# Longformer attention into a softplus MLP on one core: the second batch's v cast by its own transfers, heads paired by neighbours, and a new written-out order

## The chip, the cores and the metric

The kernel runs on one core of one Trainium2 chip. The metric is the device time of one execution in microseconds; lower is better. Five engines work side by side, each through its own instructions in order: PE (TensorE, matmuls; PEld is its weight load), DVE (VectorE), ACT (ScalarE), POOL (GpSimd) and SP (SyncE, which here only issues transfers). ACT and POOL issue transfers too. They wait for each other through semaphores.

## The reference

q, k and v have 8 batches, 8 heads, 576 tokens and 64 columns (fp32). Attention sees a window of 32 tokens to either side, and 8 global tokens that see and are seen by all. The result, put back to 4608 rows of 512, goes through a two-layer MLP with softplus.

```python
scores = scale * np.matmul(q, k.transpose(0, 1, 3, 2))
mask = np.abs(pos[:, None] - pos[None, :]) <= window
mask = mask | is_global[:, None] | is_global[None, :]
attn = softmax(np.where(mask, scores, -1e9))
x = np.matmul(attn, v).transpose(0, 2, 1, 3).reshape(B * S, H * D)
h = x @ w_in                                   # 512 -> 2048
g = np.maximum(h, 0.0) + np.log1p(np.exp(-np.abs(h)))
return g @ w_out                               # 2048 -> 512
```

## The kernel before

**Tiling.** A batch has 18 blocks of 32 queries. Four blocks make a pair-group `n` (36 in all), four groups make a stage `m` of 512 tokens (9 stages). For each group the kernel computes scores (`s`, L1077), the row maximum, the exponentials on ACT, the sum and its reciprocal, the normalised weights `pn` (L1132) and their 32x32 transposes `pt` (L1141). Once per batch the 8 global queries are scored against all keys (`sg`, L968) and applied to all values (`ov`, L997), which gives the global rows `vg`. `xo` (L1251) multiplies the weights by v, transposed, and its copies to `xT` are the MLP's input: `h` (L1286, with `w_in`, tiles `win`), softplus to `g` on ACT (L1292), and `o` (L1297, with `w_out`, tiles `wout`). The copies of all kinds share the helper at L720.

**The first two batches** (`EARLY = 2`) are loaded in parts of 256 tokens in their natural layout (`load_part`, parts t = 0, 1 and a tail of 64 tokens), rounded to bf16 (`kb`, `qb`), and transposed on PE (`tr`, with `pick`, which collects the global tokens). Block `a` of such a transpose holds head `a` on partitions 0 to 63 and head `a + 4` on 64 to 127. Later batches use layouts that DVE transposes. Stage 0's values are computed in three pieces (groups 0; 1 and 2; 3), so that the MLP can start after the first.

**Array tiles.** A score matmul is 64x32: row group `g` (64 rows), column quarter `quad(a)`. Row group 0 writes one PSUM bank and row group 1 another:

```python
for a_ in range(HG):
    for g in range(2):
        a = a_ ^ g
        nc.tensor.matmul(out=PS["s", n, g][quad(a), x, :], lhsT=qx[b % 2][rows(g), a, ...], ...)
```

So eight matmuls in a row use eight different tiles of the array. `ov` of batch 0 takes its 32-row quarters to four tiles on the array's diagonal, all into one bank; `ov` of the later batches has eight tiles and two banks.

**Loads.** SP issues q and k, and v from batch 1 on. POOL issues the transfers that cast fp32 to bf16: v of batch 0, `w_in` (four tiles of three transfers each), `w_out` (four). Two one-element transfers named `trail` make SP wait: the first for the lower half of `win2`, the second for `wout0`; what stands behind them on SP starts no earlier. v of batch 1 goes to `stage2` in fp32 and is rounded to `vb1` by a copy on ACT and one on POOL.

**What sets the order.** The class `_Order` holds all pieces of work with their dependencies. A table of numbers, `ORDER`, says piece by piece which comes next and on which engine; the class's costs only date them. Where its dates leave PE idle before `WARM`, it puts in `warm` matmuls on zeros (L729), for a share `FILL` of the gap.

Of the kernel before, what the change touches and what calls it, by code (L numbers as in the profile page):

```python
# [20 lines left out]
class _Order:  # L21
# [23 lines left out]
    def stall(self, t, took, ins):  # L45

        held, n = 0, self.issued
        asked, need, due, last = self.fetch
        due = list(due)
        while n + ins >= min(asked, need):  # L50
            at = min(asked, need)
            here = t + held + took * max(at - n, 0) / max(ins, 1)
            if at == asked:
                due.append(here)
                asked += self.BLOCK
            else:
                ask = due.pop(0)
                took_ = max(next(x for until, x in self.SLOW if ask < until), self.backlog(ask + 1200) - ask + 2400)
# [48 lines left out]
    BEGIN = 3450  # L107
    PACKETS = {1: 1024, 2: 256, 4: 576, 8: 1152}

    def settle(self, dma):  # L110
# [5 lines left out]
        while any(at[q] < len(lines[q]) for q in range(2)):  # L116
            on = []
            for q in range(2):
                if at[q] < len(lines[q]):
                    t = max(lines[q][at[q]][1], last[q])  # L120
# [30 lines left out]
    FILL, FILLT, NARROW, NFILL, NFILLT = 0.55, 220, 0, 0.8, 140  # L151
# [49 lines left out]
    def run(self, free):  # L201
# [16 lines left out]
        while ready:  # L218
# [57 lines left out]
            if j["moves"]:  # L276
                mine = "POOL" if "POOL" in j["cost"] else "SP"
                dma.append((mine, t + 1500 if j["cost"][e][0] else t, j["moves"], j))
# [28 lines left out]
def kernel(  # L307
# [45 lines left out]
    PARTED = range(4)  # L353
    LEAD = 800
# [137 lines left out]
    EARLY = 2  # L492

    hot = const([P, len(PARTS), NG], BF16, "hot")
    HD = H * D

    def flat(x):
        return x[:].rearrange("p x y z -> p (x y z)")
# [976 lines left out]
```

## Time and profile before

| | |
|---|---|
| median of 3 runs | 335.49 us (334.19 to 336.04) |
| the profiled execution | 333.06 us, of which the span on the core is 331.4 us |
| granted TensorE clock | 0.999 |
| PE busy | 317.9 us (96%), 5281 matmuls |
| DVE, ACT, POOL busy | 220.9, 231.7, 193.3 us |
| matmuls `o` and `h` | 138.6 and 136.7 us busy |
| first `h` matmul | at 27.63 us |

The span runs from the first to the last instruction; some 1.7 us of the execution lie outside it. Times in the views are counted from the span's start. PE's busy time counts the `warm` matmuls as well. A wait in brackets names what ended last before an instruction, which need not be what the instruction waited for.

### The profile page before, as it was taken

Reading aid. Unit: us, or ns where it says so; the run is one execution under the profiler, and the core shown is the slowest. Engines: PE = TensorE matmul, PEld = TensorE weight load, DVE = VectorE, ACT = ScalarE, POOL = GpSimd, SP = SyncE. Lnnn points to the kernel's source line nnn. Section 1 sums busy time; section 2 is a strip of 40 time slices with the busy share of each in tenths; the row PEclk is TensorE's granted clock in tenths of the full one; section 3 lists DMA queues with packets and bytes.
Section 4 is the critical chain, followed back from the end, with each engine's and each line's share of the span. In section 5 each row is a group of like instructions: output and inputs, shape, how many; then the busy total and the mean of one; then the engine's idle time right before and its main releaser. Section 6 shows DMA issues by size and latency. Waiting matters only on the chain.

```text
span 331.4 us, 12080 instructions
## 1 busy us (share of the span) xinstructions
PE 317.9 (96%) x5281; PEld 168.8 (51%) x5281; DVE 220.9 (67%) x387; ACT 231.7 (70%) x460; POOL 193.3 (58%) x173
## 2 busy tenths in 40 slices
PE   8778998899999999999999999999999999999995
PEld 3537874576555444544454445445544454454453
DVE  7697578786995999993895498819966890440000
ACT  5799759696897678489778947866457467925712
POOL 7865654994783596878648675496327764420000
PEclk9999999999999999999999999999999999999999
DMA  7999899898878998996994759650001112000102
GB/s 192 185 201 223 166 201 177 139 184 187 154 122 156 169 209 157 203 227 112 157 188 75 179 135 143 150 168 3 4 0 65 36 65 95 2 34 32 65 16 112
DMA packets 168860, 42.14 MB, mean 127 GB/s; under 512 B 153320, under 2 KB 165864, under 8 KB 168808
## 3 DMA queue, kind: packets, MB, share of 16 engines
q1 hardware_dynamic: 155928, 27.15, 46.0%
q0 software_dynamic: 11008, 11.08, 17.0%
q10 hardware_dynamic: 1872, 3.15, 2.5%
q8 instruction: 41, 0.67, 0.9%
q14 instruction: 11, 0.09, 0.1%
HBM read 36.71 MB, written 9.44 MB: 139 GB/s over the span
## 4 chain that ended last, share of the span: by engine, by line
PE 71%; SPq 11%; DMA 9%; ACT 4%; issue 1%; POOL 1%; DVE 1%; POOLq 0%
PE o L1297 32%; PE h L1286 29%; SPq L464 5%; PE xo L1251 4%; DMA stage<-in_q_dram 4%; SPq L469 3%; PE s L1077 3%; DMA stage<-in_k_dram 3%; ACT st L1113 2%; DMA wout<-in_moe_w_out_dram 2%; PE ov L997 1%; DMA stage<-in_v_dram 1%; SPq L518 1%; PE pick L886 1%; SPq L514 1%
## 5 line engine op out<-in xcount | busy, mean ns | idle before, releaser
L1297 PE MATMUL o<-wout,g 128*128 128x512 bf16 (+1 forms) x592 | 138.6, 374 | 0.2 <-ACT g L1292 0.2
L1286 PE MATMUL h<-xT,win 128*128 128x512 bf16 (+3 forms) x768 | 136.7, 326 | 0.8 <-DMA win<-in_moe_w_in_dram 0.8
L1292 ACT ACTIVATE g<-h 128x512 bf16<-128x512 f32 (+3 forms) x192 | 83.9, 503 | 35.0 <-PE h L1286 33.4
L1286 PEld LDWEIGHTS <-win 128*128 128x128 bf16 x768 | 66.7, 98 | 59.7 <-issue 1.1
L1132 POOL TENSOR_TENSOR pn<-st,rs 128x1024 bf16<-128x1024 f32 (+1 forms) x36 | 64.7, 1806 | 42.9 <-DVE rs L1126 38.8
L1297 PEld LDWEIGHTS <-g 128*128 128x128 bf16 x592 | 55.5, 98 | 60.6 <-ACT g L1292 1.4
L1100 POOL TENSOR_TENSOR st<-st,m 128x1024 f32<-128x1024 f32 x32 | 60.5, 1899 | 28.3 <-DVE m L1094 28.2
L1124 DVE TENSOR_REDUCE sm<-st 128x8 f32<-128x1024 f32 x32 | 38.4, 1200 | 19.0 <-ACT st L1117 18.8
L1081 DVE TENSOR_TENSOR st<-s,mask 128x512 f32<-128x512 f32 x64 | 41.3, 678 | 9.3 <-PE s L1077 9.2
L1094 DVE TENSOR_REDUCE m<-st 128x8 f32<-128x1024 f32 x32 | 38.4, 1206 | 0.4
L1117 ACT ACTIVATE st<-st 128x1024 f32<-128x1024 f32 x32 | 32.7, 1051 | 3.2 <-POOL st L1100 3.0
L1141 DVE STREAM_TRANSPOSE pt<-pn 128x512 int32<-128x512 int32 x36 | 24.6, 693 | 10.4 <-POOL pn L1132 10.2
L720 ACT COPY osb<-o 128x512 f32<-128x512 f32 (+1 forms) x27 | 15.5, 575 | 20.3 <-PE o L1297 18.7
L720 ACT CAST xT<-xo 128x512 bf16<-128x512 f32 (+3 forms) x28 | 11.5, 474 | 14.5 <-PE xo L1251 14.5
L720 POOL CAST kb<-stage 128x1152 bf16<-128x1152 f32 (+2 forms) x9 | 11.5, 1273 | 10.8 <-DMA stage<-in_q_dram 8.8
L717 POOL TENSOR_SCALAR qb<-stage 128x1152 bf16<-128x1152 f32 (+1 forms) x11 | 12.9, 1177 | 8.1 <-DMA stage<-in_q_dram 6.5
L1292 ACT ACT_TABLE_LOAD x13 | 16.7, 1283 | 0.2
L1077 PE MATMUL s<-kx,qx 64*32 64x128 bf16 x1152 | 14.7, 220 | 1.3 <-issue 0.6
L720 DVE CAST xT<-xo 128x512 bf16<-128x512 f32 (+3 forms) x20 | 11.0, 582 | 6.5 <-PE xo L1251 6.5
L1077 PEld LDWEIGHTS <-qx 64*32 64x32 bf16 x1152 | 10.0, 90 | 10.3 <-issue 7.7
L720 POOL CAST vb<-stage 128x1152 bf16<-128x1152 f32 x9 | 10.3, 1150 | 6.8 <-DVE sm L1124 3.3
L1117 ACT ACT_TABLE_LOAD x11 | 14.1, 1283 | 0.2
(129 smaller groups left out, 301.6 us busy)
## 6 DMA issues: line engine op xcount, KB each, us to landing
stage<-in_v_dram SPq DMA_DIRECT2D x56, 144.0 KB, 4.2
stage<-in_k_dram SPq DMA_DIRECT2D x48, 144.0 KB, 4.1
stage<-in_q_dram SPq DMA_DIRECT2D x48, 144.0 KB, 3.5
out_dram<-osb POOLq DMA_DIRECT2D x24, 256.0 KB, 3.6
out_dram<-osb ACTq DMA_DIRECT2D x11, 256.0 KB, 2.0
stage<-in_q_dram SPq DMA_DIRECT2D x4, 512.0 KB, 6.5
stage<-in_k_dram SPq DMA_DIRECT2D x4, 512.0 KB, 7.4
wout<-in_moe_w_out_dram POOLq DMA_DIRECT2D x4, 512.0 KB, 7.8
```

What stands on the lines that cost most here:

```text
L720: {"ACT": nc.scalar.copy, "DVE": V.tensor_copy, "POOL": nc.gpsimd.tensor_copy}[e](out, in_)
L1077: nc.tensor.matmul(out=PS["s", n, g][quad(a), x, :], lhsT=qx[b % 2][rows(g), a, j * BL:(j + 1) * BL], rhs=kx[b % 2][rows(g), a, e0 * BL:(e ...
L1081: V.tensor_tensor(out=PS["st", n][:, h, :, :], in0=PS["s", n, h][:, :, :], in1=mask[:, h, j0:j0 + PB, :, :].rearrange("p j s i -> p j (s i ...
L1094: V.reduce_max(out=m[:], in_=flat(PS["st", n], h0, h1), axis=AX)
L1100: on(e).tensor_tensor(out=t, in0=t, in1=over(PS["m", n, y][:], SL * BL), op=OP.subtract)
L1117: nc.scalar.activation(out=t, in_=t, func=AF.Exp)
L1124: V.reduce_sum(out=sm[:], in_=flat(PS["st", n], h0, h1), axis=AX)
L1132: on(e).tensor_tensor(out=PS["pn", n][:, :, :, h0:h1].rearrange("p x s h -> p h x s"), in0=PS["st", n][:, h0:h1], in1=PS["rs", n, y][:].re ...
L1141: V.transpose(out=bass.AP(base.tensor, base.offset, ap=[list(base.ap[0]), [2 * STEP, PB // 2], [STEP + BL // 2, 2], [1, SL * BL]]), in_=PS ...
L1286: nc.tensor.matmul(out=h[:, :], lhsT=w_in_t[c // 4][:, kd, c % 4 * P:(c % 4 + 1) * P], rhs=PS["xT", m][:, kd, lo:hi], start=(kd == 0), sto ...
L1292: nc.scalar.activation(out=PS["g", m, c][:, lo:hi], in_=PS[key][:, lo_of(c, hi - lo)], func=AF.Softplus)
L1297: nc.tensor.matmul(out=PS["o", m, ns, a][:, :], lhsT=PS["g", m, kf][:, ns * P:(ns + 1) * P], rhs=w_out_t[kf // 4][:, kf % 4, a:z], start=( ...
```

## The change

Six things are changed.

- v of batch 1 is no longer loaded by SP in fp32 and rounded by ACT and POOL. Eight transfers that cast, issued by POOL behind `wout3`, write `vb1` directly (`VCAST = 2`). The second `trail` now waits for `wout3`.
- In the first two batches block `a` holds heads `2a` and `2a + 1`. The tail of 64 tokens of q or k is one transfer of 64 partitions into `stage2`, and its transposes have 64 rows and all 128 columns, half as many. The new function `heads` lists which row group `g` and which column quarter `c` a head uses and which bank `h` it writes; `s` and, for these batches, `sg` follow it. `sg` there has 16 matmuls of 64 rows instead of 8 of 128.
- `win2` and `win3` become one tile `winx`, loaded by three transfers of twice the width. The first `trail` waits for the second of them.
- `FILL` goes from 0.55 to 0.8: 55 `warm` matmuls instead of 37.
- Constants by which the class dates transfers and instruction loading are changed.
- The table `ORDER` is new from the first entry to the last.

```diff
-    FILL, FILLT, NARROW, NFILL, NFILLT = 0.55, 220, 0, 0.8, 140
+    FILL, FILLT, NARROW, NFILL, NFILLT = 0.8, 220, 0, 0.8, 140
...
+    VCAST = 2
...
     ORDER = (
-        52, 57, 62, 162, 122, 137, 127, 167, 151, 146, 141, 113, 156, 132, 182, 4, 211, 117, 172, 177, 9, 241, 14, 256,
...
+    def heads(b):
+        if b < EARLY:
+            return [(2 * h + c // 2, c % 2, c, h) for h in range(2) for c in range(R)]
+        return [(a ^ g, g, a ^ g, g) for a in range(HG) for g in range(2)]
...
-            eng.dma_start(out=stage[2][quad(c), h, :, :] if b else vb[0][quad(c), :, h * D:(h + 1) * D],
+            eng.dma_start(out=vb[b][quad(c), :, h * D:(h + 1) * D] if b < VCAST else stage[2][quad(c), h, :, :],
...
+    def load_part(b, w, t, e=0):
+        if t == FULL:
+            cast_ = (b, w) in CASTS
+            (nc.gpsimd if cast_ else nc.sync).dma_start(
+                out=(rounded(w, t, 0) if cast_ else natural(w, t)).rearrange("p (h d) -> p h d", d=D),
+                in_=SRC[w][b, :, FULL * NTOK:, :].rearrange("h s d -> s h d"))
...
-    w_in_t = [wts.tile([P, KD, WC], BF16, tag=f"win{i}", name=f"win{i}") for i in range(4)]
+    w_in_t = [wts.tile([P, KD, WC], BF16, tag=f"win{i}", name=f"win{i}") for i in range(2)]
+    w_in_x = wts.tile([P, KD, 2 * WC], BF16, tag="winx", name="winx")
+    w_in_t += [w_in_x[:, :, i * WC:(i + 1) * WC] for i in range(2)]
...
-                    last = T["half", 0, h] = o.add({"POOL": (1300, 0)}, lambda e, h=h, x=x: load_v(nc.gpsimd, 0, h, range(2 * x, 2 * x + 2)), [last], rank=0,
+                    last = T["half", b, h] = o.add({"POOL": (1300, 0)}, lambda e, h=h, x=x: load_v(nc.gpsimd, b, h, range(2 * x, 2 * x + 2)), [last, *(had(("w_out", KF // 4 - 1)) if b else [])], rank=0,
...
+            def emit(e):
+                if b == EARLY:
+                    follow(1, w_out_t[KF // 4 - 1])
+                load_qk(nc.sync, b, w, (0, 2, 1, 3))
...
+                n = P if t < FULL else D
+                nc.tensor.transpose(out=ps[:, e, a, 0:n], in_=x[:, a * P:(a + 1) * P], identity=ident[0:n, 0:n])
...
+                for a, g, c, h in heads(b) if b < EARLY else [(a, None, a, 0) for a in range(HG)]:
+                    at_ = slice(0, P) if g is None else rows(g)
+                    rhs = kx[i][at_, a, (2 + 3 * a0) * BL:(2 + 3 * (a0 + an)) * BL].rearrange("p (c x) -> p c x", c=an)[:, :, 0:D]
+                    nc.tensor.matmul(out=PS["sg", b, x][quad(c), 0:an * D], lhsT=qg[i][at_, a, :], rhs=rhs, start=h == 0, stop=h == 1 or g is None)
...
-                for a_ in range(HG):
-                    for g in range(2):
-                        a = a_ ^ g
-                        nc.tensor.matmul(out=PS["s", n, g][quad(a), x, :], lhsT=qx[b % 2][rows(g), a, j * BL:(j + 1) * BL],
+                for a, g, c, h in heads(b):
+                        nc.tensor.matmul(out=PS["s", n, h][quad(c), x, :], lhsT=qx[b % 2][rows(g), a, j * BL:(j + 1) * BL],
...
-    for x in range(4):
+    for x in range(3):
```

Three places show how the order moves. The first is SP from the first `trail` on, before:

```order
L757 DMA trail<-win_126 1x2x1
L514 DMA stage_60<-in_q_dram 128x8x128
L514 DMA stage_61<-in_k_dram 128x8x128 x2
L514 DMA stage_60<-in_q_dram 128x8x128
L518 DMA stage_61<-in_k_dram 64x4x64 x2
L518 DMA stage_60<-in_q_dram 64x4x64 x2
L757 DMA trail<-wout_128 1x2x1
L469 DMA stage_62<-in_v_dram 32x18x64 x8
L464 DMA stage_61<-in_k_dram 32x36x32 x8
L464 DMA stage_60<-in_q_dram 32x36x32 x8
```

and now (stage_60 takes q, stage_61 k, stage_62 v):

```order
L770 DMA trail<-winx 1x2x1
L530 DMA stage_61<-in_k_dram 128x8x128
L530 DMA stage_60<-in_q_dram 128x8x128
L523 DMA stage_62<-in_k_dram 64x8x64
L530 DMA stage_61<-in_k_dram 128x8x128
L530 DMA stage_60<-in_q_dram 128x8x128
L523 DMA stage_62<-in_q_dram 64x8x64
L477 DMA stage_62<-in_v_dram 32x18x64 x4
L770 DMA trail<-wout_129 1x2x1
L472 DMA stage_61<-in_k_dram 32x36x32 x8
L472 DMA stage_60<-in_q_dram 32x36x32 x8
```

The parts of batch 1 stand behind a later piece of `w_in`; the eight v transfers of batch 1 are gone, and half of batch 2's v stands in front of the second `trail`, which is behind all of `w_out`.

The second place is POOL from the first v transfer to the last `w_in` transfer, before:

```order
L469 DMA vb_66<-in_v_dram 32x18x64 x8
L1370 COPY seen<-stage_60 128x1
L1350 DMA win_124<-in_moe_w_in_dram 128x2x512
L1353 DMA win_124<-in_moe_w_in_dram 64x2x512 x2
L1350 DMA win_125<-in_moe_w_in_dram 128x2x512
L1353 DMA win_125<-in_moe_w_in_dram 64x2x512 x2
L1350 DMA win_126<-in_moe_w_in_dram 128x2x512
L663 COPY mask<-mask 128x2x256
L1353 DMA win_126<-in_moe_w_in_dram 64x2x512 x2
L1350 DMA win_127<-in_moe_w_in_dram 128x2x512
L1132 TENSOR_TENSOR pn<-st,rs 128x512
L1353 DMA win_127<-in_moe_w_in_dram 64x2x512 x2
```

and now:

```order
L733 CAST kb<-stage_61 128x512
L477 DMA vb_66<-in_v_dram 32x18x64 x4
L1400 COPY seen<-stage_60 128x1
L1380 DMA win_123<-in_moe_w_in_dram 128x2x512
L1383 DMA win_123<-in_moe_w_in_dram 64x2x512 x2
L477 DMA vb_66<-in_v_dram 32x18x64 x4
L1380 DMA win_124<-in_moe_w_in_dram 128x2x512
L1383 DMA win_124<-in_moe_w_in_dram 64x2x512 x2
L1380 DMA winx<-in_moe_w_in_dram 128x2x1024
L1383 DMA winx<-in_moe_w_in_dram 64x2x1024 x2
L1161 TENSOR_TENSOR pn<-st,rs 128x512 x4
```

Half of batch 0's v stands behind `win0`, and no `pn` stands between the `w_in` transfers any more.

The third place is ACT from the first exponentials of the program to the first softplus, before:

```order
L1113 ACTIVATE st,sm<-s,m 128x128 x8
L720 COPY qx_68<-tr 128x4x128
L1113 ACTIVATE st,sm<-s,m 128x128 x4
L720 COPY qx_68<-tr 128x4x64
L1113 ACTIVATE st,sm<-s,m 128x128 x4
L980 ACTIVATE pg<-sg,gnb 128x5x2x32
L980 ACTIVATE pg<-sg,gnb 128x4x2x32
L1113 ACTIVATE st,sm<-s,m 128x128 x8
L1008 ACTIVATE vg_74<-ov,grs 128x128
L1113 ACTIVATE st,sm<-s,m 128x128 x4
L720 CAST xT<-xo 128x128 x3
L1113 ACTIVATE st,sm<-s,m 128x128 x4
```

and now:

```order
L1142 ACTIVATE st,sm<-s,m 128x128 x8
L1011 ACTIVATE pg<-sg,gnb 128x5x2x32
L1011 ACTIVATE pg<-sg,gnb 128x4x2x32
L1142 ACTIVATE st,sm<-s,m 128x128 x20
L733 CAST xT<-xo 128x128 x2
L1142 ACTIVATE st,sm<-s,m 128x128 x4
```

The same 32 exponentials; two `qx` copies, the scaling of `vg` and one `xT` copy have gone to DVE.

More of the change, by code (lines that the diff above doesn't have):

```diff
@@ L57, in stall @@
                 ask = due.pop(0)
-                took_ = max(next(x for until, x in self.SLOW if ask < until), self.backlog(ask + 1200) - ask + 2400)
+                took_ = max(next(x for until, x in self.SLOW if ask < until), self.backlog(ask + 2500) - ask + 2400)
                 last = max(ask + took_, last + self.FETCH)
@@ L119, in settle @@
                 if at[q] < len(lines[q]):
-                    t = max(lines[q][at[q]][1], last[q])
+                    t = max(lines[q][at[q]][1] + (0 if q else done[q] * self.ISSUE), last[q])
                     if q and len(gone[q]) >= deep:
@@ L277, in run @@
                 mine = "POOL" if "POOL" in j["cost"] else "SP"
-                dma.append((mine, t + 1500 if j["cost"][e][0] else t, j["moves"], j))
+                dma.append((mine, t + step + 1700 if e == "POOL" else t + 1500 if j["cost"][e][0] else t, j["moves"], j))
                 j["at"] = t
@@ L353 @@
     PARTED = range(4)
+    VCAST = 2
+    CASTS = ()
     LEAD = 800
@@ L495 @@
     HD = H * D
+    rest = [stage[2][:].rearrange("p x y z -> p (x y z)")[:, w * HD:(w + 1) * HD] for w in range(2)]
+    short = [stage[2][:].rearrange("p x y z -> p (x y z)")[:, (4 + w) * HD // 2:(5 + w) * HD // 2].bitcast(BF16) for w in range(2)]
     def flat(x):
@@ L541 @@
     count(pt_[:, 0:2 * FULL], [[NTOK, FULL], [1, 2]], 0, 2)
-    for g in range(2):
-        count(pt_[rows(g), 2 * FULL:], [[0, 1]], FULL * NTOK, 1)
+    count(pt_[:, 2 * FULL:], [[0, 1]], FULL * NTOK, 1)
     count(pos[:, P:], [[1, S - P]], P, 0)
@@ L759, in add_load @@
     def add_load(b, w, deps):
-        behind = had(("w_out", 0)) if b == 1 else []
+        behind = []
         deps = [*deps, *behind]
-        if w == 2 and not b:
+        if w == 2 and b < VCAST:
             last = None
-            T["cast", 0, 2] = []
+            T["cast", b, 2] = []
             for h in range(2):
                 for x in range(2):
-                    last = T["half", 0, h] = o.add({"POOL": (1300, 0)}, lambda e, h=h, x=x: load_v(nc.gpsimd, 0, h, range(2 * x, 2 * x + 2)), [last], rank=0,
-                                                   moves=1400, late=1600 if h else 300)
-                    T["cast", 0, 2].append(last)
-            T["load", 0, 2] = last
+                    last = T["half", b, h] = o.add({"POOL": (1300, 0)}, lambda e, h=h, x=x: load_v(nc.gpsimd, b, h, range(2 * x, 2 * x + 2)), [last, *(had(("w_out", KF // 4 - 1)) if b else [])], rank=0,
+                                                   moves=1100, late=300)
+                    T["cast", b, 2].append(last)
+            T["load", b, 2] = last
         elif w == 2:
@@ L779, in add_load, with emit @@
         else:
-            T["load", b, w] = o.add({"DMA": (4400, 0)}, lambda e: load_qk(nc.sync, b, w, (0, 2, 1, 3)), deps, rank=0, units=2 * R,
-                                    moves=8400 if b == EARLY else 9500, late=LATE, behind=had(("load", b - 1, 2)) if b == EARLY else [])
+            def emit(e):
+                if b == EARLY:
+                    follow(1, w_out_t[KF // 4 - 1])
+                load_qk(nc.sync, b, w, (0, 2, 1, 3))
+            T["load", b, w] = o.add({"DMA": (4400, 0)}, emit, deps + (had(("w_out", KF // 4 - 1)) if b == EARLY else []), rank=0, units=2 * R,
+                                    moves=8400 if b == EARLY else 9500, late=LATE)
     def add_parts(b):
-        last = None
+        last = [None, None]
         for x, (w, t) in enumerate(FIRST[b]):
-            def emit(e, x=x, w=w, t=t):
-                if b:
-                    follow(0, w_in_t[2])
-                load_part(b, w, t)
-            T["part", b, w, t] = o.add({"DMA": (700 if b else 0, 0)}, emit, had(("w_in", 2)) + T["cast", 0, w] if b else [], rank=0,
-                                       moves=(1800 if b else 1900) if t < FULL else 900 if b else 650, units=1 if t < FULL else 2)
+            for e in range(2 if t < FULL else 1):
+                if (b, w) in CASTS:
+                    was = had(("tr", 0, w, t, e)) if b else []
+                    last[0] = T["part", b, w, t, e] = o.add({"POOL": (720, 0)}, lambda eng, w=w, t=t, e=e: load_part(b, w, t, e), [last[0], *was, *(had(("w_in", 3)) if b else [])],
+                                                            rank=0, moves=1000 if t < FULL else 600, late=300)
+                elif e:
+                    T["part", b, w, t, e] = last[1]
+                else:
+                    def emit(eng, x=x, w=w, t=t):
+                        if b:
+                            follow(0, w_in_t[2])
+                        load_part(b, w, t)
+                    last[1] = T["part", b, w, t, e] = o.add({"DMA": (700 if b else 0, 0)}, emit, had(("w_in", 2)) + T["cast", 0, w] if b else [], rank=0,
+                                                         moves=(1800 if b else 1900) if t < FULL else 650, units=1)
     def add_cast(b, w):
@@ L872, in trev @@
             keys = near_keys(0, 2 * BL)
+            give = scaled if (b, w) in CASTS and not w else copy
             if t == FULL:
-                copy(eng, keys[:, :, 4 * t, :] if w else qx[i][:, :, t * NTOK:], ps[:, :, 0:D])
+                give(eng, keys[:, :, 4 * t, :] if w else qx[i][:, :, t * NTOK:], ps[:, :, 0:D])
             elif w:
@@ L919, in add_prep @@
                 for e in range(2 if t < FULL else 1):
-                    n = HD if t < FULL else HD // 2
+                    n = HD
                     was = had(("tr", b - 1, w, t, e)) if b else []
-                    job = o.add({"POOL": (110 + n, 180 + n), "ACT": act(n, False), "DVE": dve(n, False)},
-                                lambda eng, w=w, t=t, e=e: cast(eng, w, t, e), [T["part", b, w, t], *gate, *was], rank=at, port=True)
+                    if (b, w) in CASTS:
+                        job = T["part", b, w, t, e]
+                    else:
+                        job = o.add({"POOL": (110 + n, 180 + n), "ACT": act(n, False), "DVE": dve(n, False)},
+                                    lambda eng, w=w, t=t, e=e: cast(eng, w, t, e), [T["part", b, w, t, e], *gate, *was], rank=at, port=True)
+                        T["cast", b, w].append(job)
                     last = T["last", w]
@@ L1019, in add_global @@
         lead = 0 if b else LEAD
-        T["sg", b] = o.add({"PE": (270, 400) if b else (400, 530)}, sg, [x for y in T["turn", b, 1] for x in (y if b < EARLY else [y])] + had(("fill", b), ("gev", b)) + gate, rank=3, array=32, ins=16,
+        T["sg", b] = o.add({"PE": (270, 400) if b else (400, 530)}, sg, [x for y in T["turn", b, 1] for x in (y if b < EARLY else [y])] + had(("fill", b), ("gev", b)) + gate, rank=3, array=64 if b < EARLY else 32, ins=32 if b < EARLY else 16,
                            opens=[("sg", key) for key in keys], lead=lead)
@@ L1369 @@
     last = None
-    T["held"] = o.add(pool(190), lambda e: nc.gpsimd.tensor_copy(seen[:, 1, :], natural(0, 1)[:, 0, 0, 0, 0:1]), [T["part", 0, 0, 1]], rank=0, hold=300)
-    for x in range(4):
+    T["held"] = o.add(pool(400), lambda e: nc.gpsimd.tensor_copy(seen[:, 1, :], natural(0, 1)[:, 0, 0, 0:1]), [T["part", 0, 0, 1, 0]], rank=0, hold=300)
+    for x in range(3):
         for y in range(2):
-            last = T["w_in", x] = o.add({"POOL": (1300 if y else 650, 0)}, lambda e, x=x, y=y: weights_in(x, y), [last or T["held"]],
-                                        rank=-1 if x else 0, hold=2000 if x else 0, moves=1475)
+            last = T["w_in", x] = o.add({"POOL": (1250 if y else 720, 0)}, lambda e, x=x, y=y: weights_in(x, y), [last or T["held"]],
+                                        rank=-1 if x else 0, moves=2850 if x == 2 else 1425)
+    T["w_in", 3] = last
     setup("make_neg", lambda e: make_neg(), pool(1250), [], rank=0)
```

76 lines of the change are left out of this document (35 added, 41 removed), and 143 rows, old and new, of the table ORDER.

## The prediction

> **What bounds the kernel now.** I read the page's share of the span and its slices first.
>
> ```profile
> span 331.4 us, 12080 instructions
> PE 317.9 (96%) x5281; PEld 168.8 (51%) x5281; DVE 220.9 (67%) x387; ACT 231.7 (70%) x460; POOL 193.3 (58%) x173
> PE   8778998899999999999999999999999999999995
> ```
>
> PE is busy almost always; no other engine passes 70%. The 96% is a mean, so the busy time by stretch comes next, cut at the first `h`, at the end of the loads' rush, and ahead of the end. The columns are the stretch, its length, then busy time and count for PE, PEld, DVE, ACT, POOL, then clock, DMA share and GB/s.
>
> ```profile
> 0.00:27.60 27.60, 21.02 (x401) 10.61 (x402) 21.52 (x70) 22.12 (x82) 21.23 (x46) 1.00 1.32 183
> 27.60:70.00 42.40, 39.30 (x891) 28.45 (x891) 32.45 (x54) 32.48 (x91) 27.79 (x29) 1.00 1.03 185
> 70.00:318.00 248.00, 247.81 (x3963) 124.69 (x3949) 166.93 (x265) 174.92 (x285) 144.25 (x100) 1.00 0.56 114
> ```
>
> From 70 to 318 us PE loses 0.2 us. There no order can win anything, and one that makes PE wait there costs that wait in full. Between 27.6 and 70 us PE loses 3.1 us. Before 27.6 us it has 6.58 us without work, and the 21.02 us of work hold 37 `warm` matmuls that compute nothing. So the time is: when the first `h` comes, plus PE's work from there, plus what PE loses up to 70 us. Each edit is priced by these three. The clock is 1.00 in all of them.
>
> What sets the first `h` is read from the timeline (start, duration, engine, line, tiles, count, and in brackets the idle time before).
>
> ```profile
> 26.22 0.61 PE L729 MATMUL warm<-vb 128*128 128x512 bf16 x2
> 26.93 0.65 ACT L720 CAST xT<-xo 128x128 bf16<-128x128 f32 x3
> 27.63 2.84 PE L1286 MATMUL h<-xT,win 128*128 128x128 bf16 x48 [0.81 <-DMA win<-in_moe_w_in_dram]
> ```
>
> The bracket names `win`, but ACT's three `xT` casts end at 27.58, right ahead of 27.63: `h` needs all four blocks of `xT`, so I take the casts for the release.
>
> **The change part by part.** The sum is made against the profiled execution, 333.06 us (331.4 us of span and 1.66 us around it). The median is 335.49, so 2.43 us are added to compare with it.
>
> *The first `h`.* Now its first eight matmuls read `win1` and the next eight `winx`; both halves of `winx` are one tile, so its last transfer must have landed. These rows of POOL, and the time to landing of line 1353's transfers between 24 and 26 us, show how it stood before.
>
> ```profile
> 20.33 0.71 POOL L1350 DMA_DIRECT2D win<-in_moe_w_in_dram  x1
> 23.46 1.04 POOL L1132 TENSOR_TENSOR pn<-st,rs 128x512 bf16<-128x512 f32 x1 [2.42 <-DVE rs L1126]
> 24.45 1.24 POOL L1353 DMA_DIRECT2D win<-in_moe_w_in_dram  x2
> DMA to landing us min/median/max: 3.8/4.0/4.2
> ```
>
> The last two pieces were held behind a `pn` until 24.45 and landed by 29.3 (25.07 + 4.2). They belong to `win3`, which only `h` behind these 48 matmuls reads, so this cost nothing. Now no `pn` stands between, and `winx` is needed eight matmuls (8 x 2.84 / 48 = 0.47 us) behind the first. Its landing I estimate from two sides: 27.7 if POOL's 3.4 idle us between 21.04 and 24.45 are worth half (29.3 - 1.6); 30.3 if the transfers of doubled width land one us later than the single ones. The old transfers were short of DMA rather than of POOL (the share column reads 1.32 up to 27.6), so I take 28.4. With `xT` ready near 27.8 (two of its casts are now on DVE, two on ACT behind one exponential more), `h` starts at 27.8, reaches `winx` at 28.3 and loses 0.1 there. First `h` and this wait together: **+0.4 us**, bounds -0.3 (`xT` a cast earlier) and +2.2 (`winx` at 30.3 against 28.1).
>
> *The array tiles.* In the first two batches neighbouring heads use four distinct tiles where eight were used. Three rows carry the cost, two of them with the row behind.
>
> ```profile
> 15.45 0.42 PE L1077 MATMUL s<-kx,qx 64*32 64x128 bf16 x32
> 15.80 0.40 PE L857 MATMUL tr<-ident,qb 128*128 128x128 bf16 x4
> 19.19 0.43 PE L968 MATMUL sg<-kx,qg 128*32 128x320 bf16 x8 [1.49 <-DVE qg L720]
> 19.55 0.60 PE L1070 MATMUL s<-mask,ident 128*128 128x512 bf16 x2
> 22.81 1.23 PE L997 MATMUL ov<-vb,pgt 32*32 32x129 bf16 x72 [0.99 <-DVE pgt L987]
> 23.97 1.25 PE L729 MATMUL warm<-vb 128*128 128x512 bf16 x5
> ```
>
> 32 matmuls of 128 columns on eight tiles, four rounds, hold PE 0.35 us (15.45 to 15.80). 72 of 129 columns on four tiles, 18 rounds, hold it 1.16. With one switching cost w and one price r for a round, 4r + w = 0.35 and 18r + w = 1.16, so r = 0.058 and w = 0.12. On four tiles the 32 matmuls need eight rounds: +0.23 us for a pair-group. Five pair-groups of batch 1 stand behind the first `h`, in PE's full stretch: +1.15. `sg` has 2 rounds in 0.36 us, so 0.12 a round with the same w; sixteen matmuls of 64 rows make four rounds, +0.24. **+1.4 us**; the bounds are 0, if two neighbours overlap after all, and 2.0, if there is no switching cost and a round of `s` is a fourth of 0.35 (five times 0.35, and 0.24). Batch 0's stand among PE's idle time.
>
> [...] Both row groups now write one bank. [...]
>
> *The tails.* A tail has four transposes and four picks instead of eight and eight.
>
> ```profile
> 36.86 0.39 PE L857 MATMUL tr<-ident,kb 128*128 128x128 bf16 x4
> 37.18 0.38 PE L857 MATMUL tr<-ident,kb 128*128 128x128 bf16 x4
> 38.68 0.31 PE L860 MATMUL tr<-ident,kb 64*64 64x64 bf16 x8
> 39.03 0.61 PE L1286 MATMUL h<-xT,win 128*128 128x256 bf16 x4
> ```
>
> The old tail holds PE 0.35 us (38.68 to 39.03), four whole transposes and picks 0.32 (36.86 to 37.18). The new ones stand between half of the one and all of the other, 0.175 and 0.32; I take 0.22. Two tails: **-0.25 us** (-0.35 to -0.06).
>
> *SP behind the first `trail`.*
>
> ```profile
> 25.02 0.73 SPq L757 DMA_DIRECT2D trail<-win  x1
> ```
>
> It was released at 25.02; now it waits for a piece behind all of `win0` and `win1`, two thirds of `winx`, which I put at 27.1. Batch 1's parts start 2.1 us later, but a tail is one transfer instead of two, and they no longer meet the late `win3`. The `tr` of these parts stand among `h` that can fill: **+0.1 us**, from -0.4 to +1.0.
>
> *v of batch 1.* A cast of 1.14 us leaves ACT (and one POOL). What stands behind it is read from ACT's row and from the waits of PE.
>
> ```profile
> 53.95 1.14 ACT L720 CAST vb<-stage 128x1152 bf16<-128x1152 f32 x1
> PE xo L1251 <- ACT osb L720: 0.4, 1, 0.4
> PE xo L1251 <- ACT g L1292: 0.4, 1, 0.4
> ```
>
> `xo` waited twice for a PSUM bank that ACT emptied, and ACT's copies were late by less than the cast. Both go: **-0.8 us**; +0.5 at the other end, if DVE, which takes copies over, is late there instead (v itself too late is a rival). POOL issues eight transfers for it, behind the last `wout`:
>
> ```profile
> 6.20 5.53 POOL L469 DMA_DIRECT2D vb<-in_v_dram  x8
> 48.62 0.77 POOL L1357 DMA_DIRECT2D wout<-in_moe_w_out_dram  x1
> 59.55 0.80 PE L997 MATMUL ov<-vb,pgt 32*32 32x129 bf16 x72
> ```
>
> The eight of batch 0 hold POOL 5.53 us. From 49.4 they would last to 54.9, which POOL's idle time takes in (27.79 busy of 42.40), and land near 59: 54.9 plus the 4.0 above. `ov` stood at 59.55. So it fits only just; if `wout3` is issued earlier, there is room.
>
> *Waits for nothing shown.*
>
> ```profile
> 47.16 0.68 PE L1077 MATMUL s<-kx,qx 64*32 64x128 bf16 x56 [0.58 <-issue]
> 52.81 0.43 PE L968 MATMUL sg<-kx,qg 128*32 128x320 bf16 x8 [1.00 <-issue]
> ```
>
> These two stand exactly 128 matmuls apart, and a new piece of the instructions seems to be due at each. The number of instructions on PE is the same within four, so the boundaries stay, but fall elsewhere. PE eats 128 short matmuls faster than 128 long ones; of the 1.58 us I keep half: **-0.8 us**, from -1.6 to +1.5 (both at `s`, at 1.5 us each).
>
> *Fills.* 18 more `warm` at 11.57 us / 37 = 0.31 us need 5.6 of the 6.58 idle us before `h`:
>
> ```profile
> 0.00:27.60 27.60, 11.57 (x37) 3.66 (x37) 1.00 1.32 183
> ```
>
> They lie beside the loads: **0**; without that cover up to 1 us. *The order from 70 us on*: 0, and up to +2, since there is only 0.2 us to win.
>
> The sum: 0.4 + 1.4 - 0.25 + 0.1 - 0.8 - 0.8 = +0.05 us, so 333.1 for the profiled execution and **335.5 us** beside the median. 0.5% (1.7 us) is about what a measurement of this kernel can tell from no change.
>
> **The rivals.**
>
> *Faster.* The waits between 27.6 and 70 us all go (3.1 us, the second row by stretch), `xT` comes a cast earlier (-0.3), and tiles and tails cost their 1.15: -2.25 us, **333.2**; where tiles overlap, 331.8. For it: these waits have varied releasers, none of which is a limit of PE. Against it: the work behind them is the same, and the parts of batch 1 come later.
>
> *Slower: `winx` lands late.* If transfers of doubled width land at 30.3, PE stands 2.2 us at its ninth `h`, and the `trail` and all of batch 1's parts are pushed by as much (+1.0): 335.5 + 1.8 + 0.9 = **338.2**. It decides from a landing of 29.6 on. For it: a tile needs three transfers whole, and the old last pieces landed at 29.3. Against: they were held by `pn`.
>
> *Slower: row tiles in one bank go in series.* 32 matmuls in series take 32 x 0.058 + 0.12 = 1.98 us, +1.63 a pair-group, +8.1 for five; `sg` 16 x 0.12 = 1.9, +1.7: 335.5 - 1.4 + 9.8 = **344**. `ov` speaks against it.
>
> *v too late: the change doesn't do what it says.* If the v transfers, behind `wout3` and halves of batch 2's v, land 3 us behind `ov`'s place, PE waits 3 us, or POOL holds `st` behind the issues: **338.5**.
>
> **How the numbers follow.** Forecast 0.40, faster 0.36, late `winx` 0.16, series 0.04, late v 0.04. Faster by over 0.5% is 0.36, the same 0.40, slower 0.24. The likeliest case alone spans 333.9 to 337.1; the range reaches down to the faster rival with overlapping tiles and some of the loads' gain, 331.3, and up over late `winx` and late v, 339.0. Out are the series and what lies beyond either end, under 2 in 10.
>
> **What would show it.** First `h` between 27.6 and 28.2, with no gap at the ninth; `s` on 32 matmuls 0.58 us start to next start, not 0.35 or 1.98; no `xo` waiting for `osb` or `g` near 64 us; the SP parts from 27 us on; "issue" waits at other matmuls, 128 apart. A PE gap longer than 0.5 us behind 70 us, or a first `h` above 28.5, would make it wrong on the slow side; a stretch from 28 to 70 us without gaps on the fast one.

## The result: slower by 3.4%

The changed kernel takes 345.27 us (median of 4, 344.04 to 347.32) beside 335.24 us before: a ratio of 1.0338, with a 95% interval of 1.0289 to 1.0388. Forecast were 335.5 us. The profiled execution is the slowest of the four (347.32 us, span 345.6 us), so its trace shows some 2 us more than the median. Times here and below are medians of all runs of a kernel; the ratios leave out the few that fell into a slower state.

These are the page's first rows, of the changed kernel:

```profile
span 345.6 us, 12040 instructions
PE 325.9 (94%) x5283; PEld 175.2 (51%) x5283; DVE 227.3 (66%) x402; ACT 229.8 (66%) x448; POOL 200.2 (58%) x180
PE   8888469997999999999999999999999999999996
PEclk9999969999899999999999999999999999999999
```

What PE waited for there, in us, how often, and the longest:

```profile
PE tr L882 <- POOL qb L730: 7.5, 1, 7.5
PE xo L1280 <- DVE pt L1170: 2.7, 1, 2.7
PE xo L1266 <- issue: 2.3, 1, 2.3
```

The same stretches as before (PE's busy time is the first number behind the length, the clock the third from the end):

```profile
27.60:70.00 42.40, 34.65 (x685) 26.38 (x684) 24.53 (x45) 25.36 (x82) 22.24 (x29) 0.92 1.00 154
70.00:318.00 248.00, 244.65 (x4122) 124.36 (x4120) 180.47 (x289) 175.14 (x281) 158.43 (x110) 0.99 0.58 114
```

Between 27.6 and 70 us PE loses 7.8 us instead of 3.1, and the granted clock falls to 0.92 there. From 70 us on it loses 3.4 us instead of 0.2, and 0.99 of the clock is left. What the change won is outweighed: one wait of 7.5 us stands in the middle of the stretch in which the forecast was even.

The rows around it, of PE, POOL and SP:

```profile
46.15 0.61 PE L882 MATMUL tr<-ident,qb 128*128 128x128 bf16 x4 [7.49 <-POOL qb L730]
...
44.89 0.61 POOL L733 CAST stage<-stage 64x512 bf16<-64x512 f32 x1 [11.42 <-DMA stage<-in_v_dram]
45.48 0.61 POOL L730 TENSOR_SCALAR qb<-stage 128x512 bf16<-128x512 f32 x1
...
30.64 1.12 SPq L523 DMA_DIRECT2D stage<-in_k_dram  x1
34.39 2.25 SPq L523 DMA_DIRECT2D stage<-in_q_dram  x1
41.17 1.96 SPq L477 DMA_DIRECT2D stage<-in_v_dram  x4
```

PE waits for a `qb` that POOL makes in 0.61 us. POOL is late because it stands for 11.42 us ahead of another rounding, `stage<-stage`: the k tail of batch 1, which SP had asked for at 30.64. What it waits for is named: v. That is v of batch 2, in the same buffer `stage2`, asked for at 41.17, behind the q tail. In the program's text the writes and reads of `stage2` stand in this order (partitions and fp32 columns):

```
SP    k tail of batch 1       -> stage2[0:64, 512:1024]
SP    q tail of batch 1       -> stage2[0:64, 0:512]
SP    v of batch 2, quarter 0 -> stage2[0:32, 0:1152]
SP    v of batch 2, quarter 1 -> stage2[32:64, 0:1152]
SP    v of batch 2, quarter 2 -> stage2[64:96, 0:1152]
SP    v of batch 2, quarter 3 -> stage2[96:128, 0:1152]
POOL  rounding of the k tail  :  stage2[0:64, 512:1024] -> stage2[0:64, 1280:1536]
ACT   rounding of the q tail  :  stage2[0:64, 0:512]    -> stage2[0:64, 1024:1280]
```

The load of batch 2's v depends on no other piece of work (`[]` in `add_load` for that batch), and pieces are emitted by date, so it was put ahead of the roundings. They then read behind the wrong writer: they wait for v, and they round v. In the changed kernel, therefore, the scores of batch 1's last 64 tokens are of other data. The rounded q tail is also written over columns 1024 to 1151 of v, which are the last 64 tokens of heads 0 and 1 of batch 2. The amount of work is the same.

### The profile page after: what moved, and what is told of

Read it like the earlier page. It is cut to its first block, busy times and chain, and to the rows that moved or that the text cites. A ratio compares the mean times of both kernels' runs of the same rounds, so it can differ in the third digit from the quotient of the medians.

```text
span 345.6 us, 12040 instructions
## 1 busy us (share of the span) xinstructions
PE 325.9 (94%) x5283; PEld 175.2 (51%) x5283; DVE 227.3 (66%) x402; ACT 229.8 (66%) x448; POOL 200.2 (58%) x180
## 4 chain that ended last, share of the span: by engine, by line
PE 86%; DMA 5%; DVE 4%; SPq 2%; issue 1%; ACT 1%; POOL 0%
PE o L1326 36%; PE h L1315 35%; PE xo L1280 4%; PE s L1106 4%; DMA stage<-in_q_dram 2%; PE ov L1028 2%; DMA stage<-in_k_dram 2%; SPq L530 1%; PE tr L882 1%; PE pick L904 1%; DVE pick L604 1%; DMA stage<-in_v_dram 1%; PE warm L742 1%; PE sg L999 1%; ACT st L1142 1%
## 5 line engine op out<-in xcount | busy, mean ns | idle before, releaser
L1161 POOL TENSOR_TENSOR pn<-st,rs 128x1024 bf16<-128x1024 f32 (+1 forms) x38 | 67.2, 1776 | 27.2 <-DVE rs L1155 22.5
L1315 PE MATMUL h<-xT,winx 128*128 128x512 bf16 (+3 forms) x384 | 74.5, 327 | 0.0
L1315 PE MATMUL h<-xT,win 128*128 128x512 bf16 (+3 forms) x384 | 71.5, 327 | 0.0
L1315 PEld LDWEIGHTS <-winx 128*128 128x128 bf16 x384 | 33.8, 98 | 29.1
L1315 PEld LDWEIGHTS <-win 128*128 128x128 bf16 x384 | 33.6, 98 | 29.3 <-issue 0.2
L733 DVE CAST xT<-xo 128x512 bf16<-128x512 f32 (+3 forms) x23 | 12.4, 571 | 10.7 <-PE xo L1280 10.6
L733 POOL CAST kb<-stage 128x1152 bf16<-128x1152 f32 (+1 forms) x11 | 15.2, 1414 | 6.3 <-DMA stage<-in_k_dram 6.1
L1338 POOL DMA_DIRECT2D out_dram<-osb x24 | 13.8, 575 | 7.1 <-ACT g L1321 4.8
L742 PE MATMUL warm<-vb 128*128 128x512 bf16 x55 | 15.2, 429 | 1.3 <-DVE vb L562 1.3
L1106 PE MATMUL s<-kx,qx 64*32 64x128 bf16 x1152 | 16.0, 219 | 0.2 <-issue 0.2
(133 smaller groups left out, 333.8 us busy)
```

The source lines that it names most:

```text
L733: {"ACT": nc.scalar.copy, "DVE": V.tensor_copy, "POOL": nc.gpsimd.tensor_copy}[e](out, in_)
L1106: nc.tensor.matmul(out=PS["s", n, h][quad(c), x, :], lhsT=qx[b % 2][rows(g), a, j * BL:(j + 1) * BL], rhs=kx[b % 2][rows(g), a, e0 * BL:(e ...
L1161: on(e).tensor_tensor(out=PS["pn", n][:, :, :, h0:h1].rearrange("p x s h -> p h x s"), in0=PS["st", n][:, h0:h1], in1=PS["rs", n, y][:].re ...
L1315: nc.tensor.matmul(out=h[:, :], lhsT=w_in_t[c // 4][:, kd, c % 4 * P:(c % 4 + 1) * P], rhs=PS["xT", m][:, kd, lo:hi], start=(kd == 0), sto ...
```

## The experiments

### The load behind the tails

The edit leaves each engine's own order as it is:

```diff
-    for job in o.run(dict(PE=1200 if WARM else 3000, ACT=2600, DVE=2100, POOL=3400, DMA=2200)):
+    jobs = o.run(dict(PE=1200 if WARM else 3000, ACT=2600, DVE=2100, POOL=3400, DMA=2200))
+    half = T["half", 2, 0]
+    jobs.remove(half)
+    jobs.insert(1 + max(jobs.index(T["tr", 1, w, FULL, 0]) for w in range(2)), half)
+    for job in jobs:
         job["emit"](job["on"])
```

> The changed kernel, with the four transfers of the second batch's... of batch 2's v put behind batch 1's tails in the program's text; every engine's own order stays the same, only what waits for what changes (in the changed kernel batch 2's v is written over the tails before they are rounded, so the scores of those 64 tokens are of other data; here they are of the right data). Theory A, the 7.49 us without work on PE at 46.15 come from the rounding of the k tail on POOL, which waits for two transfers of batch 2's v in the same buffer: the wait goes, and with it the half clock behind it (2.3 us), so 345.3 - 7.5 - 2.3 = 335.5 us; the first h stays at 30.2. Theory B, PE waits there for instructions (it is matmul 607, 256 behind the one at which it waited at 27.47): the wait stays, 344 us or more.

Measured: 338.51 us beside 333.57, a ratio of 1.0131 (1.0090 to 1.0171). Some 60% of the loss are gone, and theory B with them. POOL and PE of this kernel:

```profile
35.46 0.61 POOL L733 CAST stage<-stage 64x512 bf16<-64x512 f32 x1 [3.78 <-DMA stage<-in_k_dram]
...
27.93 0.61 PE L1315 MATMUL h<-xT,win 128*128 128x128 bf16 x8 [0.64 <-ACT xT L733]
28.37 0.61 PE L1315 MATMUL h<-xT,winx 128*128 128x128 bf16 x8
...
36.72 0.40 PE L882 MATMUL tr<-ident,qb 128*128 128x128 bf16 x4 [0.36 <-POOL qb L730]
```

The rounding now waits for its own k tail and comes at 35.46 instead of 44.89; PE's wait shrinks from 7.49 to 0.36. The expectation was wrong in one point: the first `h` came at 27.93, not 30.2, though nothing ahead of it was changed. The wait on "issue" ahead of it varies from execution to execution: it stands at the same matmul (351) in all five profiled kernels with 55 whole `warm` matmuls and takes 2.34 us in the changed kernel, 0.18 here, and 1.86, 1.21 and 1.35 in x4_after_busy, x5_behind_pick and x8_pick_tiles. Where it was longest (2.34 and 1.86), the first `h` came at 30.23 and 30.09, in the others by 27.93.

### Fewer warm matmuls

```diff
-    FILL, FILLT, NARROW, NFILL, NFILLT = 0.8, 220, 0, 0.8, 140
+    FILL, FILLT, NARROW, NFILL, NFILLT = 0.55, 220, 0, 0.8, 140
```

> The kernel of x1_behind with FILL 0.55 as before (37 warm matmuls instead of 55). Theory A, the fills cost: they bring matmul 351 (where PE waited 2.34 us for nothing shown) forward, and nine of them stand between the last xT cast (29.49) and the first h (30.23). With fewer, the first h comes at 28.3 instead of 30.2: 1.9 us less than x1_behind. Theory B, fills lie beside the loads and cost nothing: within 0.5 us of x1_behind, the first h at 30.

Measured: 342.6 us, 1.0258 (1.0216 to 1.0301), four us slower than the kernel it was made from, with the first `h` at 27.89 (the third one waits until 28.50 for a cast on DVE). Neither theory said that. (With these dates the class puts in 46 warm matmuls, nine fewer than 55, not 37.) The trace has two waits that the other kernel has not, both inside `xo`:

```profile
144.68 0.53 PE L1280 MATMUL xo<-pt,vb 32*64 32x96 bf16 x43 [1.18 <-issue]
...
276.86 0.28 PE L1280 MATMUL xo<-pt,vb 32*64 32x64 bf16 x22 [1.47 <-issue]
```

Where the matmuls can be counted through the program, PE's longer waits on "issue" begin within four matmuls of a number 95 + 128 k: 863, 2655 and 4831 here, 863 and 991 in x1_behind, 351 in the changed kernel. At each such number a new block of instructions seems to begin. The changed kernel's page has, for its 5283 matmuls and as many weight loads, 41 transfers of instructions in one queue, one for some 258 instructions or 129 matmuls:

```profile
q8 instruction: 41, 0.67, 0.8%
```

One of them lies inside PE's wait at matmul 351 (25.13 to 27.47 us), none in the five us ahead of it. Nine matmuls fewer in front put every boundary nine matmuls later in the work. The theory to test: PE asks for a block 159 matmuls ahead, and where those 159 are short, the block is late. This distance is an estimate, fitted to the traces, which show when a block comes but not when it is asked for; it also stands among the constants by which the class of both kernels dates instruction loading (`NEED` 448 less `ASK` 130 is 318 instructions, two for each matmul).

### The same warm time in more instructions

Two kernels test it. In the kernel before, each warm matmul is split in two:

```diff
-        for x in range(n):
-            nc.tensor.matmul(out=ps[:, 0:w], lhsT=idle[:, 0, :], rhs=idle[:, 0, :] if thin else idle, start=True, stop=True)
+        for x in range(2 * n):
+            nc.tensor.matmul(out=ps[:, 0:2 * P], lhsT=idle[:, 0, :], rhs=idle[:, 0:2, :], start=True, stop=True)
```

> The kernel before, with each of the 37 warm matmuls of 512 columns split in two of 256: the same busy time of PE in front of the first h, but 37 matmuls (74 instructions) more, so that every later boundary of 128 matmuls falls 37 matmuls earlier in the work. Theory A, a block of 256 instructions is asked for 159 matmuls ahead of its use and takes 4.5 us or more to come (7 in the loads' rush), so PE waits where the 159 are short ones: counted in the trace of before, the 159 then take 4.3 us at 44, 3.4 at 141, 1.5 at 170, 2.8 at 205 and 4.5 at 236 us, which gives waits of about 2.5, 1, 3, 1.7 and 0.3 us there, and a halved clock behind the long ones: 6 to 11 us more than before. Theory B, waits for nothing shown have no place of their own: no change.

Measured: 346.21 us beside 332.69, 1.0384 (1.0341 to 1.0426): some 13 us for 74 more instructions on zeros, in front of the first `h`, with nearly the same busy time of PE (12.2 us of `warm` instead of 11.6). Theory B falls; theory A had the size too small. (Its 4.5 and 7 us for a block to come are estimates, like the 159 matmuls: where PE waited, these matmuls and the wait together took 4.3 us in x4_after_busy, 115.08 to 119.39, and 6.6 in the kernel before, 40.54 to 47.16.) Four of the waits, from PE's timeline:

```profile
47.91 0.20 PE L1250 MATMUL xo<-pt,vb 32*64 32x32 bf16 x3 [2.41 <-issue]
...
144.79 1.46 PE L1285 MATMUL h<-xT,win 128*128 128x512 bf16 x6 [2.55 <-issue]
...
178.10 0.39 PE L1076 MATMUL s<-kx,qx 64*32 64x128 bf16 x10 [2.70 <-issue]
...
248.95 0.29 PE L1250 MATMUL xo<-pt,vb 32*64 32x96 bf16 x22 [1.92 <-issue]
```

The stretches around the third:

```profile
174.00:178.00 4.00, 1.40 (x150) 1.20 (x138) 3.73 (x6) 3.27 (x4) 1.50 (x1) 0.99 0.64 139
178.00:182.00 4.00, 3.57 (x19) 1.47 (x21) 3.69 (x5) 1.38 (x2) 1.56 (x1) 0.58 0.28 63
```

Counted in the same way, the six waits of over 1 us in this trace behind the first `h`, and the four of x4_after_busy (below) behind 70 us, begin two to seven matmuls ahead of a number 95 + 128 k. The ten traces hold some 320 such places behind 70 us. At about 18 of them the 150 matmuls ahead took less than 4 us, the wait itself left out; twelve of these have a wait on "issue" of 0.45 to 3.4 us, and none of the 300 others has one over 0.4 us.

Each of the four shown stands in or right behind short matmuls (`s`, `xo`), and the clock falls to 0.58 behind the third, which makes it dearer than its 2.70 us.

In the kernel with 46 warm matmuls, the first nine were split, so that all later numbers are those of x1_behind again:

```diff
+    split = [9]
...
         for x in range(n):
+            parts = 1
+            if split[0]:
+                parts, split[0] = 2, split[0] - 1
+            for y in range(parts):
...
```

> The kernel of x2_behind_fill (46 warm matmuls), with nine of them split in two of 256 columns, so that the first h is again the matmul of the same number as in x1_behind (55). Theory A (the boundaries of 128 matmuls): the waits of 1.4 and 1.7 us inside xo at 144.7 and 276.9 us, which x2_behind_fill has and x1_behind has not, go away, a ratio to before of 1.013 as x1_behind. Theory B, fewer fills in front cost by themselves, by the clock or otherwise: 1.026 as x2_behind_fill.

Measured: 339.66 us, 1.0178 (1.0143 to 1.0214), between the two. The waits at 144 and 277 us are gone, as theory A said; the time is below that of x2_behind_fill beyond both intervals, and its interval meets that of x1_behind. Part of what is left is the clock behind a wait of 2.67 us near 79 us that all three kernels have (make_pick, below). From 70 to 120 us it is 0.97 in the profiled executions of this kernel and of x2_behind_fill, and 1.00 in that of x1_behind, some 1.5 us. The stretch behind the wait, in this kernel:

```profile
80.00:84.00 4.00, 3.50 (x121) 2.39 (x122) 3.13 (x5) 2.24 (x5) 4.00 (x4) 0.60 1.10 282
```

So the boundaries explain more than half of the four us; whether fewer fills cost something besides is open.

### PE kept busy during the wait

One group of four `h` matmuls ahead of the waiting `tr` is issued 18 times:

```diff
-            for kd in range(KD):
+            for kd in list(range(KD)) * again[0]:
...
+        again[0] = 18 if job["n"] == T["tr", 1, 1, 0, 0]["n"] + BUSY else 1
         job["emit"](job["on"])
```

> The changed kernel, with one group of four h matmuls ahead of the transposes at which PE stood issued 18 times instead of once, which takes 17 x 0.43 = 7.4 us of the wait of 7.49 us (the result of these four is the same). Theory A, the granted clock of 0.50 from 44 to 50 us follows from PE standing still: it stays at 1.00, the wait itself stays in length, and the time falls by 2.3 us to 343.0. Theory B, the clock falls there for another reason: no change, 345.3.

Measured: 360.19 us, 1.0788 (1.0744 to 1.0832). As a time this says nothing of the clock, since 68 matmuls more moved all the boundaries behind (waits on "issue" of 2.7 to 3.4 us at 119, 159 and 196 us). Its place does say it. The stretches 44 to 46 and 46 to 50 us, first of the changed kernel, then of this one:

```profile
44.00:46.00 2.00, 0.00 (x0) 0.00 (x0) 0.00 (x0) 0.00 (x0) 1.11 (x2) 0.50 0.51 95
46.00:50.00 4.00, 3.85 (x46) 3.50 (x47) 2.46 (x5) 2.08 (x4) 3.96 (x8) 0.50 0.42 46
```

```profile
44.00:46.00 2.00, 2.00 (x26) 1.83 (x25) 0.00 (x0) 0.00 (x0) 1.88 (x5) 1.00 0.20 40
46.00:50.00 4.00, 3.17 (x81) 2.67 (x81) 2.75 (x5) 2.67 (x5) 3.97 (x7) 1.00 0.57 84
```

With PE standing, the granted clock is 0.50; with PE kept busy, 1.00. The price is read from the `tr` on `qb` at which PE stood (46.15 in the changed kernel) to the next `s`, which holds the same matmuls in both. The `s` of the changed kernel, then both rows of this one:

```profile
50.48 1.07 PE L1106 MATMUL s<-kx,qx 64*32 64x128 bf16 x64
...
45.91 0.38 PE L882 MATMUL tr<-ident,qb 128*128 128x128 bf16 x4
...
48.55 0.45 PE L1106 MATMUL s<-kx,qx 64*32 64x128 bf16 x18
```

It takes 4.33 us in the one and 2.64 in the other: the half clock costs 1.7 us, not 2.3. In the changed kernel the clock stands at 0.50 from 43.47 to 50.29 us: it falls 4.8 us behind PE's last work (38.66) and comes back 4.1 us behind the `tr` at 46.15. A shorter wait does this at times. Behind the 2.67 us ahead of `xo` the changed kernel's clock fell, that of x1_behind did not:

```profile
88.00:92.00 4.00, 4.00 (x64) 1.80 (x51) 2.69 (x5) 2.79 (x5) 3.98 (x5) 0.59 1.11 279
```

```profile
80.00:84.00 4.00, 3.84 (x108) 2.32 (x109) 2.75 (x5) 3.12 (x6) 3.99 (x4) 1.00 1.19 285
```

### The wait that was left: make_pick

In x1_behind PE still waits 2.67 us for `pt` at 79.02. DVE and POOL ahead of it, then `place` and the same four comparisons in the kernel before:

```profile
71.59 1.86 DVE L599 TENSOR_SCALAR place<-pos,pi 128x32 bf16<-128x32 f32 x1
71.62 1.83 DVE L600 TENSOR_SCALAR pi<-pi 128x1 f32<-128x1 f32 x1
...
73.75 3.27 DVE L604 TENSOR_TENSOR pick<-posK,gf 32x144 bf16<-32x144 f32 x4
77.06 0.71 DVE L1170 STREAM_TRANSPOSE pt<-pn 128x512 int32<-128x512 int32 x1
...
71.51 1.90 POOL L1161 TENSOR_TENSOR pn<-st,rs 128x1024 bf16<-128x1024 f32 x1
73.35 2.94 POOL L733 CAST kb<-stage 128x1152 bf16<-128x1152 f32 x2
...
79.02 0.37 PE L1280 MATMUL xo<-pt,vg 32*64 32x384 bf16 x6 [2.67 <-DVE pt L1170]
```

```profile
73.61 0.24 DVE L588 TENSOR_SCALAR place<-pos,pi 128x32 bf16<-128x32 f32 x1
...
74.20 1.24 DVE L593 TENSOR_TENSOR pick<-posK,gf 32x144 bf16<-32x144 f32 x4
```

The set-up work takes 5.7 us (71.4 to 77.1) where it took 2.0 before, and `pt` stands behind it. It was moved to where DVE waits for `sg`:

```diff
+    jobs.remove(T["make_pick"])
+    jobs.insert(jobs.index(T["mxg", 1]), T["make_pick"])
```

> The kernel of x1_behind, with the set-up work make_pick (seven DVE instructions, 71.4 to 77.1 us there) put ahead of batch 1's gm on DVE, where DVE waits for sg anyway. Theory A, it is what PE waits for at 79.0 (2.67 us, named DVE pt): its four comparisons take 0.30 us each in the kernel before (73.4 to 75.4 us in all) and up to 1.44 beside POOL's casts of kb, and two pt transposes stand behind it. The wait goes: 2.7 to 3.2 us less than x1_behind, a ratio to before of 1.004. Theory B, pt is late because of POOL's pn, which stands ahead of it: the wait stays, 1.013 as x1_behind.

Measured: 335.62 us beside 332.69, 1.0081 (1.0056 to 1.0106). The wait is gone. The profiled span fell from 336.3 to 333.8 us, the ratio by 0.5%, less than expected (the two intervals overlap). Part of the gain is lost in new waits: DVE comes to `gm` at 59.00 instead of 57.31, and PE waits 0.54 us ahead of `ov` at 64.36 and 0.33 ahead of `o` at 68.19, where x1_behind has none. The four comparisons take their 1.24 us again, but `place` is long in its new place too:

```profile
55.41 1.91 POOL L1129 TENSOR_TENSOR st<-st,m 128x1024 f32<-128x1024 f32 x1
...
55.74 1.63 DVE L599 TENSOR_SCALAR place<-pos,pi 128x32 bf16<-128x32 f32 x1
57.73 1.24 DVE L604 TENSOR_TENSOR pick<-posK,gf 32x144 bf16<-32x144 f32 x4
...
76.73 0.38 PE L1280 MATMUL xo<-pt,vg 32*64 32x384 bf16 x8
```

That theory A is right in what PE waited for is shown. Why DVE was slow beside POOL is read from the rows alone: `place` ends with POOL's `pn` in x1_behind (73.45 and 73.41) and with POOL's `st` in x5_behind_pick (57.37 and 57.32), and the comparisons are slow until `kb` is done (up to 1.44 us; the last, begun at 76.7 behind `kb`'s end at 76.29, takes 0.30). No run here tests why.

### The array tiles, from both sides

In the kernel before, `s` of the first two batches on four tiles, row groups mixed in one bank:

```diff
+                order = [(2 * h + c // 2, c % 2, c, h) for h in range(2) for c in range(R)] if b < EARLY else [(a_ ^ g, g, a_ ^ g, g) for a_ in range(HG) for g in range(2)]
+                for a, g, c, h in order:
```

> The kernel before, with the score matmuls of the first two batches on four array tiles, both row groups into one bank, as in the change (the scores of these batches are then of other heads; size and number of matmuls stay). Prediction's term: five pair-groups behind the first h at +0.23 us, so +1.15 us, 336.4 us. Rival, neighbours overlap all the same: 335.2 us. Rival, row groups into one bank go in series: +8 us, 343 us.

Measured: 333.39 us beside 333.57, 0.9994 (0.9959 to 1.0029): no difference. The rows show both why the price was right and why it was not paid:

```profile
31.80 0.68 PE L1250 MATMUL xo<-pt,vb 32*64 32x96 bf16 x61 [0.92 <-issue]
...
41.49 0.63 PE L1076 MATMUL s<-kx,qx 64*32 64x128 bf16 x32
42.05 0.40 PE L857 MATMUL tr<-ident,qb 128*128 128x128 bf16 x4
...
48.43 0.96 PE L1076 MATMUL s<-kx,qx 64*32 64x128 bf16 x56 [0.26 <-issue]
```

32 matmuls hold PE 0.56 us (41.49 to 42.05) instead of 0.35. But the wait of 0.58 us in the next but one `s` is 0.26 now, that of 1.00 us ahead of `sg` is gone, and by 66 us the `xT` copies are level with those before (65.92 and 66.03). This execution even lost 0.92 us more on "issue" at 31.80, where the kernel before has no wait. So in these rows longer matmuls only fill a wait; that the coming of instructions sets the pace there is my reading of them, which no run tests. Then the reverse, in the repaired change:

```diff
-                for a, g, c, h in heads(b):
+                for a, g, c, h in [(a ^ g, g, a ^ g, g) for a in range(HG) for g in range(2)]:
```

> The kernel of x5_behind_pick, with the score matmuls of the first two batches on eight tiles and two banks in turn, as before (the scores of these batches are then of other heads; size and number stay). It is the test of x3_before_tiles from the other side. Theory A, four tiles cost their 0.21 us a pair-group here: five behind the first h, 1.05 us less than x5_behind_pick, a ratio to before of 1.005. Theory B, what they save is taken up by the waits for instructions behind them, as x3_before_tiles showed no difference: 1.008.

Measured: 335.80 us beside 333.39, 1.0065 (1.0029 to 1.0100). The interval holds both theories. In the traces 0.3 to 0.4 us of the 1.05 are kept by 69 us, as the wait ahead of `o` at 54.93 grew from 0.22 to 0.92 us.

## Why the prediction was wrong

*The step that failed* is "SP behind the first `trail`: +0.1 us, from -0.4 to +1.0". It dated batch 1's parts by the `trail` alone. The order quoted ahead of the prediction shows four v transfers into `stage_62` right behind the tails' two; I read them as late loads and did not ask which write of the buffer the tails' roundings come behind. Nor could `h` fill the gap: in PE's order no `h` stands between the work that ends at 38.66 and the `tr` at 46.15. From there a wait of 7.49 us follows, and some 1.7 us of half clock. Undoing that alone takes the ratio from 1.0338 to 1.0131, about 6.9 us.

*The order from 70 us on*, "0, and up to +2", was mis-sized: the order puts `make_pick` beside POOL's long instructions, PE waits 2.7 us, and moving it takes 2.5 us off the span and 0.5% off the ratio.

*Waits for nothing shown*, -0.8: the places were right (128 matmuls apart), the sign not. In x1_behind they are 1.6 and 0.8 us, in the kernel before 0.6 and 1.0. That they take up a saving or a loss of the work around them was not seen.

*The first `h`*, +0.4: 27.93 in x1_behind, +0.3, with no gap at the ninth (28.37 is 0.44 behind). The changed kernel's own profile had 30.23, beyond the upper bound of +2.2, by a wait on "issue" of 2.34 us. *The tiles*, +1.4: the price is right (0.56 for 32, and `sg` 0.60 for 16), the sum is not, since up to 53 us the waits on "issue" took it up in x3_before_tiles (0.58 to 0.26, 1.00 to none); the term cannot be told from nothing. *The tails*, -0.25: with 64 rows a tail takes 0.30 us (38.32 to 38.62 in x1_behind) instead of 0.35, so -0.1. *v of batch 1*, -0.8: no `xo` waits for `osb` or `g` near 68 us in x1_behind, so these waits went. *Fills*, 0: their time lies beside the loads but for the changed kernel's own profile, where the last nine end some 0.7 us behind the last `xT` cast (29.49); but each moves every later boundary, which the working did not count.

*The rivals.* Late `winx` did not happen; row groups in one bank went side by side (0.56 us for 32 matmuls in x3_before_tiles, not 1.98); v of batch 1 was in time. The measured 345 us lie beside the 344 of the series, by another mechanism. "The change doesn't do what it says" was given for the wrong v: it was v of batch 2 that came, too early in the text. Both signs that were named for the slow side show in the changed kernel's trace (the first `h` at 30.23, a gap of 2.67 us behind 70 us); the wait that cost most was on no list.

*What stays open.* x5_behind_pick is still 2.7 us slower than before. Its trace has 4.8 us of waits from 27.6 to 318 us (short gaps between `o` matmuls, where records are missing, left out) against 3.2, and with 1.2 for tiles and tails and 0.2 for the first `h` (27.84) that comes to about 3.0; but x8_pick_tiles leaves the tiles' share unsettled. No version faster than the kernel before was found.

## What to carry to other kernels

When a change lets two transfers share a buffer, list its writers and readers in the order of the program's text, across engines: a rounding that stood behind the wrong writer waited 11.42 us for it here, and what stood behind it on its engine did too. Count instructions as well as time where an engine runs short matmuls: dummy work in idle time was not free here (some 13 us for 37 more matmuls in x6_before_split), as it shifted the places at which PE waited on "issue". And before a saving on PE is added up, ask whether a wait behind it takes it.

## What was not expected of the hardware

37 more matmuls on zeros, at nearly the same busy time, cost some 13 us, all of it behind the first `h`, in waits of up to 2.7 us that stand multiples of 128 matmuls apart, within five, and in a lower clock behind one (0.58 from 178 to 182 us). A DVE instruction of 32 numbers a partition (`place`) took 1.86 and 1.63 us beside POOL instructions of 1.90 and 1.91 and ended with them; in the kernel before it took 0.24.
